# Moving the loads of attention's keys, values and queries from SyncE's queue to GpSimd's

## The chip, the cores and the metric

The kernel runs on one core of one Trainium2 chip. Times are device microseconds of a whole execution; the median of three runs is compared. A profiled execution gives, beside its own device time, a trace whose times count from the first instruction of the span.

## The reference

`q`, `k`, `v` are (8, 8, 576, 64) in float32: 8 sequences, 8 heads, 576 tokens, 64 columns. Retention (linear attention with a decay and no softmax) is followed by a feed-forward layer with a softplus:

```python
scores = q @ k.T / sqrt(64)
ret = (scores * Dmat) @ v            # Dmat[i, j] = gamma[h] ** (i - j) for i >= j, else 0
x = ret, its heads side by side      # 4608 tokens x 512
h = x @ w_in                         # 512 -> 2048
g = max(h, 0) + log1p(exp(-abs(h)))
out = g @ w_out                      # 2048 -> 512
```

## The kernel before

**Attention in steps.** The 4608 tokens are 36 chunks of 128. A step `m` is half a chunk's heads, so there are 72 steps, two to a chunk. A step's data are a `keys` tile (128x512 float32, 256 KB: the keys in two layouts) and a `qv` tile (128x640, 320 KB: queries and values). Steps 0 to 10 are loaded whole into tiles of their own. From step 11 on `load_keys` and `load_rest` issue two DMAs for each step, into two buffers for `keys` and two for `qv` (odd steps from 17 on have their `qv` in a pool named `odd`, so that there are then four).

**What a step does.** `chunk_products` gives TensorE a group of small 64x64 matmuls: scores (L204) and sums of key times value (L220) of the coming step or pair of steps, values (L282) and the terms from the running state (L294) of the one before. GpSimd copies half of the old state into `sx` (L259), multiplies the new state by its decay (L278) and scales the values of a loaded step by a power of gamma (L197, `scale_values`). L220 of a step reads those scaled values, so the order for a step is: load `qv`, land, L197, next group on TensorE. A buffer of `keys` or `qv` comes free when the group that reads it last has run.

**The feed-forward layer** is done for 512 tokens at a time (a unit), in float32 split into a high and a low part, three matmuls for one. Up to about 121 us `hidden_mm` (L453) and `output_mm` (L482) run while the weights arrive (`wst`). From then on the split weights, and sums of their blocks (Strassen's scheme: seven products for eight), lie in HBM, and each `product` (L830, six 128x512 matmuls) or `second` (L1117) takes its block from a ring of five buffers of 256 KB; `block_load` (L600) issues the load of the next block as soon as a product has been put out.

**Stages.** 42 to 121 us: hidden and output products beside the weights. 121 to 201 and 229 to 311 us: `plain_slot`, two products and a unit's outputs in each slot, a group of small matmuls in every second one. 201 to 229 and 325 to 463 us: `strassen_pair`, seven products, outputs and a group. About 517 to 624 us: the first `full_pair`s, seven products and one or two `second`s with a group in each. Then no attention is left.

**Order of issue.** Each engine runs its instructions in the order in which the program writes them. All DMAs are issued by SyncE (SP): loads of weights, ring blocks, `keys`, `qv`, and stores. In `plain_slot` the group's loads for the steps after (`next_steps`) are issued at once behind the group's matmuls. In `strassen_pair` and `full_pair`, `queue_steps` puts them into the list `queued`, of which each `product` issues one behind its ring block:

```python
load_keys(ks[0])
queued[:0] = [lambda: load_rest(ks[0]), lambda: load_rest(ks[1]), lambda: load_keys(ks[1])]
queued.append(lambda: [scale_values(k) for k in ks])
```

Of the kernel before, what the change touches and what calls it, by code (L numbers as in the profile page):

```python
# [34 lines left out]
KEYS = 4 * C  # L35
# [4 lines left out]
FIRST = AHEAD - 1  # L40
# [42 lines left out]
def retention_softplus_ffn(ctx: ExitStack, tc, first, whole, others, consts, w, out):  # L83
    nc = tc.nc
# [68 lines left out]

    def load_keys(m):
        keys = rawp.tile([P, KEYS], F32, tag="keys", name="keys")
        nc.sync.dma_start(keys, others[m - FIRST][:, 0:KEYS])
        loaded(m, k=keys[:, 0:2 * C], kp=keys[:, 2 * C:])

    def load_rest(m):
        place = later["odd"] if m >= 2 * CHUNKS - 1 and m % 2 else rawp  # L160
        qv = place.tile([P, RAW - KEYS], F32, tag="qv", name="qv")
        nc.sync.dma_start(qv, others[m - FIRST][:, KEYS:])
        loaded(m, q=qv[:, 0:-2 * C], v=qv[:, -2 * C:])

    def loaded(m, **tiles):
        live.setdefault(m, {}).update((n, x.rearrange("p (s c) -> p s c", s=2)) for n, x in tiles.items())

    def load_step(m):

        if m == 0:  # L170
            at = 0
            for x in parts:
                nc.sync.dma_start(x, first[:, at:at + x.shape[1]])
                at += x.shape[1]
            k, q = parts[0][:, 0:2 * C], parts[0][:, 2 * C:4 * C]
            kp, v = parts[1][:, 0:2 * C], parts[1][:, 2 * C:4 * C]
        else:
            if m < NOPEN:
                place = openp if m < OPEN1 else openp2
                r = place.tile([P, 8 * C if m < FIRST else RAW], F32, name=f"raw{m}")  # L180
                nc.sync.dma_start(r, whole[m - 1] if m < FIRST else others[m - FIRST])
                keys, qv = r[:, 0:KEYS], r[:, KEYS:]
            else:
                load_keys(m)
                load_rest(m)
                return
            k, kp, q, v = keys[:, 0:2 * C], keys[:, 2 * C:], qv[:, 0:-2 * C], qv[:, -2 * C:]
        live[m] = {n: x.rearrange("p (s c) -> p s c", s=2) for n, x in dict(k=k, q=q, kp=kp, v=v).items()}
# [543 lines left out]
    for i in range(NF):  # L732
        n = START_WEIGHTS + 2 * i
        m = AHEAD + (i - 1) // 2
# [72 lines left out]
    def queue_steps(steps):  # L807
        ks = [m + 2 for m in steps if m + 2 < NSTEP]
        if not ks:
            return  # L810
# [3 lines that stand above are left out]
# [560 lines left out]
```

## Time and profile before

| | us |
|---|---|
| median of three runs | 845.3 |
| the three runs | 843.07, 845.3, 846.12 |
| the profiled execution, device time | 844.79 |
| its span in the trace | 843.0 |
| TensorE busy in the span | 829.7 |
| GpSimd busy in the span | 157.5 |

The profiled execution took 1.79 us outside its span. TensorE's granted clock was 0.999 of full speed over the span. In the trace PE is TensorE's matmul, PEld its weight load, DVE VectorE, ACT ScalarE, POOL GpSimd and SPq SyncE's queue of DMA issues.

### The profile page before, as it was taken

Reading aid. Unit: us, or ns where it says so; the run is one execution under the profiler, and the core shown is the slowest. Engines: PE = TensorE matmul, PEld = TensorE weight load, DVE = VectorE, ACT = ScalarE, POOL = GpSimd, SP = SyncE. Lnnn points to the kernel's source line nnn. Section 1 sums busy time; section 2 is a strip of 40 time slices with the busy share of each in tenths; the row PEclk is TensorE's granted clock in tenths of the full one; section 3 lists DMA queues with packets and bytes.
Section 4 is the critical chain, followed back from the end, with each engine's and each line's share of the span. In section 5 each row is a group of like instructions: output and inputs, shape, how many; then the busy total and the mean of one; then the engine's idle time right before and its main releaser. Section 6 shows DMA issues by size and latency. Waiting matters only on the chain.

```text
span 843.0 us, 18984 instructions
## 1 busy us (share of the span) xinstructions
PE 829.7 (98%) x7370; PEld 674.8 (80%) x7370; DVE 602.4 (71%) x1024; ACT 536.2 (64%) x921; POOL 157.5 (19%) x212
## 2 busy tenths in 40 slices
PE   7999999999999999999999999999999999999998
PEld 6788888887888888888888888787778888888786
DVE  5999965876587667777775744877789955555875
ACT  6778754447654447667766436676775658878643
POOL 4322222440222441111101000112110002212100
PEclk9999999999999999999999999999999999999999
DMA  9898878656677763988789747879756676666665
GB/s 364 299 304 307 289 259 311 224 197 225 227 258 261 253 206 105 325 277 268 252 282 305 271 176 243 255 218 302 226 155 213 209 243 191 188 192 194 198 205 190
DMA packets 137481, 203.64 MB, mean 242 GB/s; under 512 B 10288, under 2 KB 99888, under 8 KB 137392
## 3 DMA queue, kind: packets, MB, share of 16 engines
q1 hardware_dynamic: 137392, 202.43, 72.6%
q8 instruction: 59, 0.97, 0.5%
q14 instruction: 30, 0.25, 0.1%
HBM read 156.25 MB, written 46.14 MB: 240 GB/s over the span
## 4 chain that ended last, share of the span: by engine, by line
PE 85%; DVE 5%; ACT 4%; DMA 3%; issue 1%; POOL 1%; SPq 0%; DVEq 0%; POOLq 0%; ACTq 0%
PE y L482 23%; PE acc L830 18%; PE sum L1117 12%; PE two L830 11%; PE h L453 4%; PE third L830 4%; PE third L220 2%; PE two L204 2%; PE two L1117 1%; PE two L282 1%; PE third L1117 1%; PE acc L1117 1%; DMA ring<-combined 1%; PE two L294 1%; DMA raw<-whole 1%
## 5 line engine op out<-in xcount | busy, mean ns | idle before, releaser
L482 PE MATMUL y<-wout,g 128*128 128x512 f32 x960 | 233.7, 392 | 0.2 <-DVE g L475 0.2
L482 PEld LDWEIGHTS y<-wout,g 128*128 128x128 f32 x960 | 178.5, 188 | 38.7 <-PE h L453 0.6
L830 PE MATMUL acc<-xt,ring 128*128 128x512 f32 x768 | 194.1, 391 | 0.4 <-DMA ring<-combined 0.2
L830 PEld LDWEIGHTS acc<-xt,ring 128*128 128x128 f32 x768 | 143.6, 188 | 32.7 <-ACT parts L1107 0.7
L830 PE MATMUL two<-xt,ring 128*128 128x512 f32 x480 | 122.4, 391 | 1.3 <-DVE quad L956 0.5
L1117 PE MATMUL sum<-parts,ring 128*128 128x512 f32 x480 | 118.1, 396 | 0.0
L830 PEld LDWEIGHTS two<-xt,ring 128*128 128x128 f32 x480 | 89.6, 188 | 22.0 <-ACT ab L1154 1.6
L1107 ACT CAST parts<-g 128x512 fp32r<-128x512 f32 x112 | 68.5, 621 | 60.0 <-PE sum L1117 19.4
L1117 PEld LDWEIGHTS sum<-parts,ring 128*128 128x128 f32 x480 | 89.1, 188 | 21.7 <-DMA ring<-outsplit 0.6
L1111 DVE TENSOR_TENSOR parts<-g,parts 128x512 fp32r<-128x512 f32 x112 | 78.0, 714 | 29.9 <-ACT parts L1107 28.6
L462 ACT ACTIVATE ab<-ab 128x512 f32<-128x512 f32 x128 | 81.0, 632 | 4.1
L463 ACT ACTIVATE ab<-ab 128x512 f32<-128x512 f32 x128 | 80.9, 632 | 4.1
L471 ACT CAST g<-ab 128x512 fp32r<-128x512 f32 x60 | 37.1, 619 | 57.5 <-DVE ab L467 35.8
L197 POOL TENSOR_TENSOR qv<-qv,consts_sb 128x256 f32<-128x256 f32 x61 | 45.7, 749 | 125.5 <-DMA qv<-others 125.5
L475 DVE TENSOR_TENSOR g<-ab,g 128x512 fp32r<-128x512 f32 x60 | 44.2, 737 | 16.2 <-ACT g L471 15.3
L259 POOL COPY sx<-s 64x256 f32<-64x256 f32 (+1 forms) x34 | 13.2, 389 | 207.6 <-PE third L220 161.2
L1127 DVE SCALAR_TENSOR_TENSOR g<-g,ab 128x512 f32<-128x512 f32 x64 | 45.2, 716 | 7.3 <-ACT ab L463 7.1
L453 PE MATMUL h<-xt,win 128*128 128x512 f32 x192 | 48.3, 400 | 1.0 <-DVE x L397 0.7
L278 POOL TENSOR_TENSOR s<-s,consts_sb 128x256 f32<-128x256 f32 (+1 forms) x31 | 20.3, 656 | 127.8 <-DVE s L276 111.7
L453 PEld LDWEIGHTS h<-xt,win 128*128 128x128 f32 x192 | 35.4, 188 | 9.6 <-ACT wout L563 0.8
L1213 POOL TENSOR_TENSOR g<-g 128x512 f32<-128x512 f32 x9 | 12.3, 1369 | 151.2 <-DVE g L1127 151.2
L461 ACT ACTIVATE ab<-quad 128x512 f32<-128x512 f32 x40 | 25.2, 631 | 23.4 <-DVE quad L956 12.0
(182 smaller groups left out, 1322.5 us busy)
## 6 DMA issues: line engine op xcount, KB each, us to landing
ring<-split SPq DMA_DIRECT2D x126, 256.0 KB, 3.9
ring<-combined SPq DMA_DIRECT2D x104, 256.0 KB, 3.6
qv<-others SPq DMA_DIRECT2D x61, 320.0 KB, 4.8
wst<-w SPq DMA_DIRECT2D x32, 512.0 KB, 5.8
ring<-outcombined SPq DMA_DIRECT2D x64, 256.0 KB, 3.4
keys<-others SPq DMA_DIRECT2D x61, 256.0 KB, 4.8
ring<-outsplit SPq DMA_DIRECT2D x48, 256.0 KB, 3.8
split<-win SPq DMA_DIRECT2D x16, 512.0 KB, 6.5
```

The lines of the kernel that those rows point to most:

```text
L197: nc.gpsimd.tensor_mul(v, v, f.unsqueeze(2).broadcast_to([P, 4, D]))
L453: nc.tensor.matmul(h, wins[p][:, a, kt * P:(kt + 1) * P], xt[:, b, T1 + kt // 2, kt % 2], start=(n == 0), stop=(n == 3 * NKT - 1))
L462: nc.scalar.activation(ab, ab, AF.Exp, scale=-1.0)
L463: nc.scalar.activation(ab, ab, AF.Ln, bias=1.0)
L471: nc.scalar.copy(g[:, HI], ab)
L475: nc.vector.tensor_sub(g[:, LO], ab, g[:, HI].bitcast(F32))
L482: nc.tensor.matmul(ys[u][tt], g[:, a, tt * P:(tt + 1) * P], wouts[p][:, b], start=(p == 0 and n == 0), stop=(p == NF - 1 and n == 2))
L830: nc.tensor.matmul(bank, w[:, ta, kt * P:(kt + 1) * P], xt[:, tb, x, kt], start=start and k == 0, stop=k == 5, skip_group_check=True)
L1107: nc.scalar.copy(t[:, HI], g_slot(J, n))
L1111: nc.vector.tensor_sub(t[:, LO], g_slot(J, n), t[:, HI].bitcast(F32))
L1117: nc.tensor.matmul(bank[m], w[:, a, m * P:(m + 1) * P], t[:, b], start=start and n == 0, stop=n == 2, skip_group_check=True)
L1127: nc.vector.scalar_tensor_tensor(c, c, 0.0, ab, op0=ALU.max, op1=ALU.add)
```

## The change

From step 11 on, the two loads of each step are issued by GpSimd instead of SyncE. The diff in full:

```diff
     def load_keys(m):
         keys = rawp.tile([P, KEYS], F32, tag="keys", name="keys")
-        nc.sync.dma_start(keys, others[m - FIRST][:, 0:KEYS])
+        nc.gpsimd.dma_start(keys, others[m - FIRST][:, 0:KEYS])
         loaded(m, k=keys[:, 0:2 * C], kp=keys[:, 2 * C:])
 
     def load_rest(m):
         place = later["odd"] if m >= 2 * CHUNKS - 1 and m % 2 else rawp
         qv = place.tile([P, RAW - KEYS], F32, tag="qv", name="qv")
-        nc.sync.dma_start(qv, others[m - FIRST][:, KEYS:])
+        nc.gpsimd.dma_start(qv, others[m - FIRST][:, KEYS:])
         loaded(m, q=qv[:, 0:-2 * C], v=qv[:, -2 * C:])
```

These are 122 DMAs, 61 of each kind. The order of instructions on TensorE, VectorE and ScalarE is the same before and after. Two places show what moves on the other two.

The first is GpSimd's order in the `full_pair` that begins at 534 us (tiles `keys_6539` and `qv_6553` are step 62's, `keys_6576` and `qv_6565` step 63's). Before:

```order
L259 COPY sx_6531<-s_6338 64x256
L278 TENSOR_TENSOR s_6536<-s_6536,consts_sb_101 128x256
L197 TENSOR_TENSOR qv_6553<-qv_6553,consts_sb_101 128x256
L197 TENSOR_TENSOR qv_6565<-qv_6565,consts_sb_101 128x256
L259 COPY sx_6721<-s_6536 64x256
```

After:

```order
L259 COPY sx_6531<-s_6338 64x256
L278 TENSOR_TENSOR s_6536<-s_6536,consts_sb_101 128x256
L156 DMA keys_6539<-others 128x512
L162 DMA qv_6553<-others 128x640
L162 DMA qv_6565<-others 128x640
L156 DMA keys_6576<-others 128x512
L197 TENSOR_TENSOR qv_6553<-qv_6553,consts_sb_101 128x256
L197 TENSOR_TENSOR qv_6565<-qv_6565,consts_sb_101 128x256
L259 COPY sx_6721<-s_6536 64x256
```

The four loads stand behind the state's decay L278, all in one piece. On SyncE, before, the same four loads stood one by one between ring blocks:

```order
L156 DMA keys_6539<-others 128x512
L600 DMA ring_6551<-combined2_1_124 128x2x256
L162 DMA qv_6553<-others 128x640
L600 DMA ring_6563<-combined2_1_124 128x2x256
L162 DMA qv_6565<-others 128x640
L600 DMA ring_6574<-outsplit3_138 128x2x256
L156 DMA keys_6576<-others 128x512
L600 DMA ring_6586<-split5_108 128x2x256
```

Of these rows only the four of the ring are left on SyncE.

The second place is the last `plain_slot` with a group, at 306 us, on GpSimd. After the change (before, the same rows without the four DMAs):

```order
L156 DMA keys_4001<-others 128x512
L162 DMA qv_4003<-others 128x640
L156 DMA keys_4005<-others 128x512
L162 DMA qv_4007<-others 128x640
L259 COPY sx_4009<-s_3844 64x256
L278 TENSOR_TENSOR s_4014<-s_4014,consts_sb_101 128x256
L197 TENSOR_TENSOR qv_4003<-qv_4003,consts_sb_101 128x256
L197 TENSOR_TENSOR qv_4007<-qv_4007,consts_sb_101 128x256
L434 TENSOR_TENSOR quad_4038<-xs_546 128x256
```

Here the four loads come ahead of `sx` and of the state's decay, and GpSimd's combinations of the next units' inputs (L434 to L437) stand last.

## Rows read from the trace of the kernel before

**Rows 1.** The profile's page, part 1 (busy us, share of the span, instructions of each engine) and the head of part 4 (the chain of work that ended last, share of the span by engine).
```profile
PE 829.7 (98%) x7370; PEld 674.8 (80%) x7370; DVE 602.4 (71%) x1024; ACT 536.2 (64%) x921; POOL 157.5 (19%) x212
...
PE 85%; DVE 5%; ACT 4%; DMA 3%; issue 1%; POOL 1%; SPq 0%; DVEq 0%; POOLq 0%; ACTq 0%
```

**Rows 2.** Who TensorE waited for between 42 and 843 us: us in total, times, longest us. The view has six rows; one of 0.4 us (ACT) and one of 0.7 us (issue) are left out.
```profile
PE third L220 <- DVE mark L336: 0.8, 2, 0.4
...
PE two L830 <- DVE quad L956: 0.5, 1, 0.5
...
PE two L830 <- DMA ring<-combined: 0.4, 1, 0.4
PE acc L830 <- DMA ring<-combined: 0.2, 1, 0.2
```

**Rows 3.** Busy time by stretch: us, then for each engine busy us (instructions), the granted TensorE clock, the DMA engines' share and GB/s.
```profile
42.00:121.00 79.00, 78.95 (x687) 63.36 (x687) 70.93 (x132) 61.28 (x107) 18.57 (x25) 1.00 0.84 287
...
517.00:610.00 93.00, 90.97 (x1162) 73.30 (x1163) 72.16 (x128) 66.61 (x115) 15.76 (x24) 1.00 0.79 253
```

**Rows 4.** Who SyncE's queue waited for before it issued a load of `keys`: us in total, times, longest us.
```profile
SPq L156 <- PE third L220: 22.6, 15, 2.5
```

**Rows 5.** The page, part 6: DMA issues, their count, KB each, median us from issue to landing.
```profile
ring<-combined SPq DMA_DIRECT2D x104, 256.0 KB, 3.6
qv<-others SPq DMA_DIRECT2D x61, 320.0 KB, 4.8
```

**Rows 6.** The view of the tile `qv`: SyncE's time for one issue (ns, min/median/max) and the time from issue to landing.
```profile
L162 SPq DMA_DIRECT2D qv<-others x61: 332/550/1979, 43.8 to 599.5; - x61
...
DMA to landing us min/median/max: 3.1/4.8/7.8
```

**Rows 7.** The timeline of GpSimd in the `full_pair` from 534 us: start us, us, instruction, [idle before <- what ended it].
```profile
534.70 0.39 POOL L259 COPY sx<-s 64x256 f32<-64x256 f32 x1 [4.85 <-PE third L220]
538.48 0.61 POOL L278 TENSOR_TENSOR s<-s,consts_sb 128x256 f32<-128x256 f32 x1 [3.38 <-DVE s L276]
...
543.27 0.66 POOL L197 TENSOR_TENSOR qv<-qv,consts_sb 128x256 f32<-128x256 f32 x1 [2.17 <-DMA qv<-others]
549.28 0.39 POOL L259 COPY sx<-s 64x256 f32<-64x256 f32 x1 [5.34 <-PE third L220]
```

**Rows 8.** The timeline of TensorE where the next group begins.
```profile
545.82 1.30 PE L830 MATMUL acc<-xt,ring 128*128 128x512 f32 x5
547.05 0.73 PE L204 MATMUL two<-qv,keys 64*64 64x64 f32 x21
```

**Rows 9.** The timeline of SyncE's queue in the same `full_pair`.
```profile
538.14 0.59 SPq L162 DMA_DIRECT2D qv<-others  x1
...
539.51 0.59 SPq L156 DMA_DIRECT2D keys<-others  x1
540.30 0.52 SPq L600 DMA_DIRECT2D ring<-split  x1
```

**Rows 10.** The chain of work that ended last, between 306 and 326 us: start us, us, what.
```profile
306.66 0.10 POOL sx L259
...
313.48 0.61 POOL qv L197
314.08 1.69 POOL quad L434
...
318.59 1.16 POOL quad L437
...
319.77 1.06 ACT xt L441
...
320.85 1.23 DVE xt L442
...
323.73 0.70 DVE quad L956
...
324.47 1.67 PE two L830 x6
```

**Rows 11.** The timeline of SyncE's queue, GpSimd and TensorE around the load of step 17's `qv`.
```profile
116.34 0.33 SPq L162 DMA_DIRECT2D qv<-others  x1
116.72 3.22 SPq L600 DMA_DIRECT2D ring<-split  x5
119.72 0.61 POOL L197 TENSOR_TENSOR qv<-qv,consts_sb 128x256 f32<-128x256 f32 x1 [6.65 <-DMA qv<-others]
...
120.99 0.24 PE L220 MATMUL third<-qv,keys 64*64 64x64 f32 x1
```

**Rows 12.** GpSimd's groups of instructions, shapes kept apart: count | busy us, mean ns of one.
```profile
L278 POOL TENSOR_TENSOR s<-s,consts_sb 128x256 f32<-128x256 f32 x24 | 15.3, 640 | 75.0 <-DVE s L276 67.4 <-DVE s L274 7.5
...
L434 POOL TENSOR_TENSOR quad<-xs 128x256 f32<-128x256 f32 x8 | 8.0, 994 | 0.0
```

**Rows 13.** The timeline of GpSimd: the state's decay L278 in the first, the fourth and the sixth `full_pair`, and the `sx` copies behind the fourth and the sixth.
```profile
522.93 0.61 POOL L278 TENSOR_TENSOR s<-s,consts_sb 128x256 f32<-128x256 f32 x1 [3.38 <-DVE s L276]
...
568.44 0.61 POOL L278 TENSOR_TENSOR s<-s,consts_sb 128x256 f32<-128x256 f32 x1 [3.38 <-DVE s L276]
...
579.27 0.39 POOL L259 COPY sx<-s 64x256 f32<-64x256 f32 x1 [5.36 <-PE third L220]
...
599.81 0.61 POOL L278 TENSOR_TENSOR s<-s,consts_sb 128x256 f32<-128x256 f32 x1 [3.38 <-DVE s L276]
...
610.62 0.39 POOL L259 COPY sx<-s 64x256 f32<-64x256 f32 x1 [5.35 <-PE two L294]
```

**Rows 14.** The timeline of GpSimd and TensorE in a `plain_slot`: the second scaling, a combination, and the group that reads the scaled values.
```profile
160.49 0.61 POOL L197 TENSOR_TENSOR qv<-qv,consts_sb 128x256 f32<-128x256 f32 x1 [0.98 <-DMA qv<-others]
161.06 1.18 POOL L434 TENSOR_TENSOR quad<-xs 128x256 f32<-128x256 f32 x1
...
162.53 0.27 PE L220 MATMUL third<-qv,keys 64*64 64x64 f32 x1
```

## The prediction, made before the changed kernel was run

> **What bounds the kernel now.** I read the page's shares and its chain first: TensorE is busy for 829.7 of 843.0 us and holds 85% of the chain that ended last, GpSimd 19% busy and 1% of the chain [rows 1]. So time can only be won or lost where TensorE stops. The waits of TensorE after 42 us are the next view: they come to some 3 us in all, and those that a DMA ended are 0.4 and 0.2 us, both for ring blocks [rows 2]. No wait of TensorE is for `keys` or `qv`. The table by stretch agrees: from 42 to 121 us TensorE is busy for 78.95 of 79.00 us, from 517 to 610 us for 90.97 of 93.00 [rows 3]. The reader should see that there is next to nothing to gain, and look for slack that the change could use up.
>
> **What the change takes away.** SyncE loses 122 issues of 0.55 us (median) [rows 6], and its waits ahead of them, of which the largest row is 22.6 us over 15 times [rows 4]. Behind those stood ring blocks and weight loads, which now go out earlier. That is worth at most what TensorE waited for the ring, 0.6 us [rows 2], and I count nothing for it: the chunk loads still move their bytes beside the ring's, and may make one of its blocks late as before.
>
> **What it adds.** GpSimd issues 122 DMAs, four in a row from the plain slots on. The trace has no DMA issued by GpSimd, so its price t, as time that GpSimd is held, must be bounded. Lower end: 0.33 us, SyncE's shortest issue of the same load; nothing at all is excluded, since the instruction has to be carried out in line. Upper end: 1.7 us, GpSimd's longest 128x256 instruction on the chain [rows 10]. Between them lie SyncE's median of 0.55 [rows 6] and GpSimd's own instructions, 0.64 (L278) and 0.99 (L434) on average [rows 12]. I take t = 1.0: the nearest rows are GpSimd's own, and an issue for 128 rows is more than a short elementwise instruction.
>
> The Trainium skill, DMA: Bandwidth & Descriptors, section "Latency and other measured facts", gives about 0.6 us to the first byte for a DMA of SyncE and about 1 us for one of GpSimd, whose cores write the descriptors in software. If only that difference of 0.4 us counted, each load would land 0.4 us later and the sum below would be smaller, about half a microsecond (an estimate from that page); no row here shows it.
>
> From the end of the issue to landing: SyncE's fastest is 3.1 less 0.33, some 2.8 us; its median 4.8 less 0.55, some 4.2 [rows 6], with other loads queued ahead. I take 3.5, the middle; ring blocks, of nearly the same size, land 3.6 us after issue [rows 5].
>
> **Where that meets slack.** GpSimd does its list in order, so I go through it by stage.
>
> From 42 to 116 us GpSimd issues two loads per step and has little else to do. They leave when the buffer comes free rather than behind weight loads, so they come no later; nothing.
>
> (a) *Step 17's `qv`*, the first into the memory that the weights leave. SyncE issues it at 116.34, it is scaled from 119.72 to 120.33, and TensorE starts the group at 120.99 [rows 11]: 0.66 us of slack. The memory comes free no earlier after the change, so it is 116.34 + 1.0 + 3.5 + 0.61 = 121.45, or 0.5 us late. The five ring loads, until now behind it, move beside it, a reason not to take less than 3.5.
>
> (b) *Plain slots.* Four issues come ahead of the `sx` copy and the state's decay, which are needed one group later, some 11 us on; that covers them. Without that cover it would be 4t a group. The loads themselves: in the tightest slot the second scaling ends at 161.10 and TensorE reads at 162.53 [rows 14], 1.4 us of slack. Against SyncE's issues (four of 0.55) the fourth leaves 4 x (1.0 - 0.55) = 1.8 us later, less what the queue in front then saves, 4.2 - 3.5 = 0.7: 1.1 us later. It just fits; nothing.
>
> The last plain slot has no slack. There the chain runs from the group's end on TensorE at 306.66 over the last `qv` load, its scaling at 313.48, GpSimd's combinations L434 to L437, ACT, DVE, and back to TensorE at 324.47 [rows 10], where TensorE already waits for that L956 [rows 2]. After: 306.66 + 4 x 1.0 + 3.5 = 314.16, 0.7 us later than 313.48, and TensorE with it.
>
> (c) *Strassen pairs and `full_pair`s.* Here the loads wait behind the decay L278. Of the two the `full_pair`s are tight. L278 ends at 539.09 [rows 7]; SyncE had issued the last `qv` at 538.14 and the last `keys` at 539.51 [rows 9]. Four issues end at 543.09, the last `keys` land at 546.6, the last `qv` (third) at 545.6, scaled by 546.3. TensorE starts the next group at 547.05 [rows 8]. 0.4 us to spare: nothing. Every issue over (547.05 - 539.09 - 3.5) / 4 = 1.1 us would stop TensorE in each such pair.
>
> Sum against the profiled execution: 844.79 + 0.5 (a) + 0.7 (b) = 846.0. It stands 0.5 below the median of its runs, so I forecast **846.5**, 0.14% slower, which a comparison of such runs cannot tell from no change; about 0.5% (4.2 us) is what can be told.
>
> **Rivals.**
>
> *GpSimd's issues are dear, and the next group waits* (slower). GpSimd's own instructions stretch: L434 takes 0.99 on average but 1.69 on the chain, next to a busy DVE [rows 10, 12]. If issues stretch alike, t = 1.7: from L278's start to the next `sx` copy there are 10.8 us in three `full_pair`s (538.48 to 549.28, 568.44 to 579.27, 599.81 to 610.62 [rows 7, 13]) and some 11.8 in the other three (522.93 to 534.70). The first three lose 4 x (1.7 - 1.1) = 2.4 us each, the others 1.4: 11.4. (b) becomes 3.5 and (a) 1.2, and plain slots lose a little each, so about 17 us: 862. With t = 1.4 it is 3 x 1.2 + 0.6 (others) + 2.3 + 0.9 = 7.4: 852.7. It decides from t = 1.25 on, where the sum passes 4.2 us. Against it: L278 itself, in the same place, shows 0.61 [rows 13]. The Trainium skill, SBUF — State Buffer, section "Who interferes with whom", names a mechanism: DMAs of GpSimd starve while DVE holds the port pair that both share with certain one-input instructions; by that rule t would swing with what DVE runs. The rows here show GpSimd's stretching, not its cause.
>
> *The four loads together starve the ring* (slower). They used to be spread over four products, now 1.15 MB goes out in 4t, beside ring blocks. In the `full_pair`s a product takes some 1.4 us and the ring is four ahead; a block that lands at the loads' pace (4.8 instead of 3.6 us [rows 5]) is 1.2 us later. If one in each of the six `full_pair`s that load were late by that, it would be 7.2 us: 852.5. Against it: the ring has waited behind the same bytes before and lost 0.6 us.
>
> *SyncE freed makes it faster.* All that TensorE waited for after 42 us is 3 us, the DMA part 0.6 [rows 2]: 844.7. It cannot pass 0.5%.
>
> **How the numbers follow.** Forecast 0.58; dear issues 0.27; starved ring 0.07; SyncE freed 0.08, of which I leave half to a gain that the view of waits does not show, and half is no change. So 0.04 faster, 0.62 same, 0.34 slower. The range runs from 843.5, all DMA waits gone and cheap issues, to 855, the ring's case and dear issues up to t = 1.5; about 0.17 is left outside, most of it above.
>
> **What would show it.** In the changed kernel's trace: GpSimd's DMA rows with their own time (about 1.0 us); the second L197 after 306 us starting near 314.2 and TensorE's L830 near 325; in the `full_pair`s the last scaling about 0.8 us ahead of the group. Waits of TensorE for POOL or for `qv` and `keys` in groups from 517 us on would show the first rival, with the price of an issue beside them; waits for ring blocks the second. I would be wrong if the landing after GpSimd's issue took much more than 3.5 us: each microsecond there weighs like 0.25 us of t.

## The result, and the profile after

The changed kernel takes 855.65 us (median of six runs, 853.26 to 857.33) against 845.5 us before (six runs, 843.07 to 846.12), a ratio of 1.0122 with a 95% interval of 1.0103 to 1.0141. It is 10 us slower; the forecast was 846.5, its range ended at 855.0. The profiled execution took 856.09 us, with a span of 854.4.

The page, parts 1 and 4 as in [rows 1]: TensorE's busy time has grown from 829.7 to 834.2 us, its share of the chain has fallen from 85% to 76%, and that of DMA has doubled.
```profile
PE 834.2 (98%) x7370; PEld 676.6 (79%) x7370; DVE 606.2 (71%) x1024; ACT 535.9 (63%) x921; POOL 223.5 (26%) x334
...
PE 76%; DVE 9%; DMA 6%; ACT 5%; issue 2%; POOL 1%; SPq 0%; DVEq 0%; ACTq 0%; POOLq 0%
```

Who TensorE waited for from 42 to 843 us (us in total, times, longest), as in [rows 2]. Waits for ring blocks were 0.6 us; now they are 5.4 + 0.6, and the 2.5 put down to DVE's L639 belong to them too, as the rows after next show. There is still no wait for `keys` or `qv`.
```profile
PE acc L830 <- DMA ring<-split: 5.4, 5, 2.6
PE acc L830 <- DVE quad L639: 2.5, 1, 2.5
PE two L830 <- DVE quad L956: 1.0, 2, 0.5
...
PE sum L1117 <- DMA ring<-outsplit: 0.6, 2, 0.4
```

The stretches of [rows 3] after: from 42 to 121 us TensorE is all but as busy as before (78.85 of 79.00 us), while from 517 to 610 us it is busy for 85.82 us instead of 90.97, and the DMA engines moved 221 GB/s instead of 253.
```profile
517.00:610.00 93.00, 85.82 (x1039) 68.31 (x1038) 67.05 (x116) 61.77 (x106) 23.73 (x42) 0.98 0.66 221
```

One `full_pair` shows what happens, the one of [rows 7 to 9]. First GpSimd's timeline (start us, us, instruction):
```profile
542.80 0.58 POOL L156 DMA_DIRECT2D keys<-others  x1
543.37 1.06 POOL L162 DMA_DIRECT2D qv<-others  x2
544.42 0.54 POOL L156 DMA_DIRECT2D keys<-others  x1
548.19 0.69 POOL L197 TENSOR_TENSOR qv<-qv,consts_sb 128x256 f32<-128x256 f32 x1 [3.23 <-DMA qv<-others]
549.54 0.72 POOL L197 TENSOR_TENSOR qv<-qv,consts_sb 128x256 f32<-128x256 f32 x1 [0.66 <-DMA qv<-others]
```
Then SyncE's issue of one ring block, the time from that issue to its landing (the view of line L600 at 544 us), that of the same block before the change (issued at 540.30 in [rows 9]), and TensorE's wait for it:
```profile
544.05 0.52 SPq L600 DMA_DIRECT2D ring<-split  x1
```
```profile
DMA to landing us min/median/max: 7.8/7.8/7.8
```
```profile
DMA to landing us min/median/max: 5.0/5.0/5.0
```
```profile
551.99 1.23 PE L830 MATMUL acc<-xt,ring 128*128 128x512 f32 x3 [2.50 <-DVE quad L639]
```
The ring block that left at 544.05 landed at 551.85, and TensorE went on at 551.99. The row names the combination L639, which ended just before, but the product does not need it: before the change the same product ran at 545.59, and L639 came after it, on VectorE:
```profile
547.29 0.42 DVE L639 TENSOR_TENSOR quad<-quad 128x256 f32<-128x256 f32 x1
```
Ring blocks take 3.4 to 4.4 us in the medians of the page; this one took 7.8, with four loads of GpSimd leaving around it. The loads themselves are late too, though no wait shows it: the second scaling ends at 550.26, but the last `keys`, issued at 544.42, took 7.2 us and landed at 551.64, hardly before the ring block.
```profile
DMA to landing us min/median/max: 7.2/7.2/7.2
```

Then a second cost comes, which the waits do not count. The granted clock of TensorE behind that wait, by stretches of 1 us (busy times, then the clock in the third column from the end):
```profile
552.00:553.00 1.00, 1.00 (x3) 0.78 (x4) 0.96 (x3) 0.00 (x0) 0.00 (x0) 0.72 0.56 180
553.00:554.00 1.00, 1.00 (x4) 0.66 (x2) 0.13 (x1) 0.00 (x0) 0.00 (x0) 0.50 0.09 29
554.00:555.00 1.00, 1.00 (x13) 0.57 (x14) 0.00 (x0) 0.46 (x1) 0.00 (x0) 0.50 0.01 2
555.00:556.00 1.00, 1.00 (x48) 1.00 (x47) 0.00 (x0) 0.97 (x3) 0.00 (x0) 0.57 0.04 11
```
After 2.5 us without work the clock fell to 0.50, the lower of its two levels (1.2 of 2.4 GHz). Over the four rows 0.28 + 0.50 + 0.50 + 0.43 = 1.71 us of full speed are lacking, so it was low for 3.4 us and TensorE lost some 1.7 on top of the wait. Not every such wait has this price: the longest of the trace, 2.6 us until 602.1, was followed by full clock.
```profile
602.00:603.00 1.00, 0.92 (x4) 0.83 (x5) 0.84 (x3) 0.00 (x0) 0.00 (x0) 1.00 0.41 135
```

**Where the 11.4 us between the spans lie.** The same instruction, after less before: 1.69 us by the first hidden product (rows below), 2.15 at step 17's group (123.14 - 120.99, [rows 11]), 2.53 at 324 us (327.00 - 324.47, [rows 10]), 3.21 at the first `full_pair`'s decay (526.14 - 522.93, [rows 13]) and 11.32 at the `sx` copy behind the sixth (621.94 - 610.62). So 8.1 us arose in the six `full_pair`s, 1.5 between 25 and 523 us, and 1.7 at the start. The last row, and the one at the first decay, after the change:
```profile
526.14 0.62 POOL L278 TENSOR_TENSOR s<-s,consts_sb 128x256 f32<-128x256 f32 x1 [3.39 <-DVE s L276]
```
```profile
621.94 0.39 POOL L259 COPY sx<-s 64x256 f32<-64x256 f32 x1 [4.29 <-PE two L294]
```
The waits add up to that: in the `full_pair`s TensorE waits 8.5 us for ring blocks (5.4 + 2.5 + 0.6 above) and loses 1.7 to the clock, and some 1.9 us that it waited there before are gone: 8.3, for the 8.1 of the spans.

The start is no part of the change. TensorE's first hidden product before, and after:
```profile
23.54 2.79 PE L453 MATMUL h<-xt,win 128*128 128x512 f32 x11 [0.66 <-DVE x L397]
```
```profile
25.23 3.03 PE L453 MATMUL h<-xt,win 128*128 128x512 f32 x12 [0.66 <-DVE x L397]
```
Among the kernels below this instruction started anywhere from 23.29 us (`paced`, all loads on GpSimd) over 25.08 (`only_full`, none on GpSimd until 517 us) to 25.83 (`act_spread`, none on GpSimd at all).

### The profile page after: what moved, and what is told of

Its sections match the earlier page's. It is cut to its first block, busy times and chain, and to the rows that moved or that the text cites. A ratio compares the mean times of both kernels' runs of the same rounds, so it can differ in the third digit from the quotient of the medians.

```text
span 854.4 us, 18928 instructions
## 1 busy us (share of the span) xinstructions
PE 834.2 (98%) x7370; PEld 676.6 (79%) x7370; DVE 606.2 (71%) x1024; ACT 535.9 (63%) x921; POOL 223.5 (26%) x334
## 4 chain that ended last, share of the span: by engine, by line
PE 76%; DVE 9%; DMA 6%; ACT 5%; issue 2%; POOL 1%; SPq 0%; DVEq 0%; ACTq 0%; POOLq 0%
PE acc L830 19%; PE y L482 18%; PE sum L1117 12%; PE two L830 10%; DMA ring<-split 4%; PE third L830 4%; PE two L1117 3%; PE third L220 2%; PE two L204 2%; DVE wst L551 1%; PE two L282 1%; DVE g L475 1%; PE acc L1117 1%; PE third L1117 1%; PE two L294 1%
## 5 line engine op out<-in xcount | busy, mean ns | idle before, releaser
L278 POOL TENSOR_TENSOR s<-s,consts_sb 128x256 f32<-128x256 f32 (+1 forms) x31 | 20.3, 654 | 104.3 <-DVE s L276 87.3
L156 POOL DMA_DIRECT2D keys<-others x61 | 34.3, 562 | 42.7 <-PE third L220 29.2
```

## The experiments

All are timed against the kernel before on the same chip; its medians there were 844.4 to 845.3 us. "Between 517 and 630 us" are the `full_pair`s. Steps 60 to 71 are loaded there.

### Where: late_sync and only_full

`late_sync`, and `only_full` with the condition turned round:
```diff
-        nc.gpsimd.dma_start(keys, others[m - FIRST][:, 0:KEYS])
+        (nc.gpsimd if m < 60 else nc.sync).dma_start(keys, others[m - FIRST][:, 0:KEYS])
```
and the same for `qv`.

> GpSimd issues the loads of steps 11 to 59, SyncE those of steps 60 to 71 (the full_pairs), as before the change. Theory A (the loss arises where four loads leave together beside the full_pairs' tight ring): the 8.3 us that TensorE lost between 517 and 612 us are gone, what is left is the shift of 2 to 3 us that the changed kernel shows before 517 us, so 846 to 848.5 us; no wait of TensorE over 0.3 us for a ring block in the full_pairs. Rival (GpSimd's loads cost something wherever they stand, by its issues or its queue): 850 us or more.

> SyncE issues the loads of steps 11 to 59, GpSimd only those of steps 60 to 71. Theory A: the whole loss of the full_pairs is there, 853 to 855 us, with TensorE waiting some 8 us for ring blocks between 517 and 612 us, and nothing lost before 517 us. If the first 42 us start as early as in the kernel before, the 1.7 us that the changed kernel lost there come from GpSimd's queue in use early; if they are late again, from the chance of a start or from the queue being there at all. Rival (cost wherever GpSimd issues): 847 us, a fifth of the loads having a fifth of the loss.

Measured: `late_sync` 847.52 us, ratio 1.0036 (1.0019 to 1.0053); `only_full` 855.89, ratio 1.0145 (1.0111 to 1.0178), a little more than expected. In `late_sync` the stretch from 517 to 610 us is as before (rows 3: 90.97):
```profile
517.00:610.00 93.00, 91.35 (x1070) 73.13 (x1069) 71.85 (x126) 66.65 (x115) 15.58 (x24) 1.00 0.76 248
```
Its two waits for ring blocks there, 0.5 and 0.3 us, are those of the kernel before in kind and size. What follows: 24 of the 122 loads, those of the `full_pair`s, make most of the loss. The other 98 cost 1.6 to 4.5 us.

### Four at once, or the queue: sync_burst, paced, gp_early, act_spread, sync_late

In `sync_burst` SyncE issues all loads, in the `full_pair`s the four in a row (against the kernel before):
```diff
         load_keys(ks[0])
-        queued[:0] = [lambda: load_rest(ks[0]), lambda: load_rest(ks[1]), lambda: load_keys(ks[1])]
+        if ks[0] >= 60:
+            for f in (lambda: load_rest(ks[0]), lambda: load_rest(ks[1]), lambda: load_keys(ks[1])):
+                f()
...
```
`paced` is the changed kernel with idle work ahead of the second, third and fourth load:
```diff
+        def apart(f):
+            if ks[0] >= 60:
+                for _ in range(4):
+                    t = rawp.tile([P, C], F32, tag="idle", name="idle")
+                    nc.gpsimd.memset(t, 0.0)
+            f()
-        queued[:0] = [lambda: load_rest(ks[0]), lambda: load_rest(ks[1]), lambda: load_keys(ks[1])]
+        queued[:0] = [lambda: apart(lambda: load_rest(ks[0])), lambda: apart(lambda: load_rest(ks[1])),
+                      lambda: apart(lambda: load_keys(ks[1]))]
```

> No load is issued by GpSimd. In the full_pairs SyncE issues the four loads in a row where the first of them stood before, not one by one between ring blocks. Theory A1 (four loads at once starve the ring, whoever issues them): the ring blocks behind the four land some 3 us late, 851 to 856 us. Theory A2 (it takes GpSimd's own queue, whose packets go ahead of the ring's in the DMA engines, or the later place in GpSimd's order): 845 to 848 us.

> The changed kernel, with four memsets of 128x128 on GpSimd (0.20 us each) between one load and the next in the full_pairs, so that the four leave some 1.35 us apart, about as far apart as SyncE issued them. Theory A1 (four at once): most of the 8.3 us comes back, 846 to 850 us, ring blocks at most 6.5 us from issue to landing. Theory A2 (GpSimd's queue itself): 853 to 857 us, ring blocks up to 8 us late as in the changed kernel.

Measured: `sync_burst` 849.37 us (847.06 to 853.41), ratio 1.0056 (1.0032 to 1.0079): between the two theories. `paced` 852.18, ratio 1.0097 (1.0080 to 1.0115): also between. Its loads left 1.1 to 1.5 us apart, and ring blocks still took up to 7.1 us. Its waits between 517 and 630 us, of which the second comes with the idle work (the last `keys` leave later and come too late):
```profile
PE acc L837 <- DMA ring<-split: 4.1, 5, 1.5
PE third L220 <- DMA keys<-others: 2.1, 2, 1.8
PE sum L1124 <- DMA ring<-outsplit: 1.5, 1, 1.5
```
So the bunching is part of it: four in a row on the ring's own queue already cost 4.9 us (849.37 against 844.43), about half of the loss. But neither theory holds alone. Three runs took place and queue apart. `gp_early` puts GpSimd's loads ahead of the decay (against the changed kernel):
```diff
             chunk_products(*group)
+            ks = next_steps(group[0])
             group_out(*group, between=(finish,))
-            queue_steps(group[0])
+            queued.append(lambda: [scale_values(k) for k in ks])
```
`act_spread` gives the `full_pair`s' loads to ScalarE, one behind each product (against the kernel before, `qv` alike):
```diff
-        nc.sync.dma_start(keys, others[m - FIRST][:, 0:KEYS])
+        (nc.scalar if m >= 60 else nc.sync).dma_start(keys, others[m - FIRST][:, 0:KEYS])
...
```
`sync_late` leaves them with SyncE, three products later (against the kernel before):
```diff
+        gap = 3 if ks[0] >= 60 else 0
...
+            queued[:0] = [lambda: None] * gap + [lambda: load_keys(ks[0])]
```

> The changed kernel, but in the full_pairs GpSimd issues the four loads right behind the group's matmuls, ahead of the sx copy and of the state's decay L278, so about where SyncE issued its first one and some 4 us sooner than in the changed kernel; still four in a row on GpSimd's queue. Theory P (the loss comes from the later place behind the decay, so that the loads meet the ring where its reserve is used up): 847 to 849 us. Theory Q (on GpSimd's own queue the loads pass the ring blocks that were issued before them): 851 to 856 us, and ring blocks of 6 us or more from issue to landing that left before the loads did.

> No load is issued by GpSimd. In the full_pairs ScalarE issues the four loads, one by one at the places where SyncE did, on a queue of its own. Theory Q (loads on another queue than the ring's pass ring blocks issued before them): ring blocks of 6 us and more from issue to landing in the full_pairs, 848 to 853 us. Rival (it takes GpSimd's software-made packets, or the later place): 845 to 847 us, if ScalarE's four issues of some 0.5 us per full_pair stay hidden.

> No load is issued by GpSimd. In the full_pairs SyncE issues the four loads one by one between ring blocks as in the kernel before, but three products (some 4 us) later, about where GpSimd issued them. Theory P (the later place makes the loss): 850 to 855 us. Theory Q (GpSimd's own queue makes it): 845 to 847.5 us, ring blocks at most 6 us from issue to landing.

Measured: `gp_early` 856.69 us, ratio 1.0128 (1.0101 to 1.0155); `act_spread` 854.17, ratio 1.0104 (1.0070 to 1.0139); `sync_late` 870.86, ratio 1.0299 (1.0247 to 1.0351).

`gp_early` differs from the changed kernel in the place alone and is no faster, so the place behind the decay is not the cause (theory P falls); it stands 0.7 us above the range of theory Q. It issues from 521.05 us on in the first `full_pair`, `sync_burst` from 519.79: nearly the same place, the same four in a row, another queue, and 7.3 us between them. Not all of these belong to the queue in the `full_pair`s, since `gp_early` has the other 98 loads on GpSimd too (1.6 to 4.5 us by `late_sync`). `only_full` leaves those with SyncE as `sync_burst` does: it is 6.5 us slower, and the two intervals lie apart. So a queue of its own costs more than the bunching alone. The wait row of `gp_early`, and the clock in one of the 6.8 us that it stayed low around the end of a wait of 2.9 us at 530.94:
```profile
PE acc L830 <- DMA ring<-combined: 7.0, 3, 3.0
```
```profile
531.00:532.00 1.00, 1.00 (x3) 0.81 (x4) 0.00 (x0) 0.00 (x0) 0.00 (x0) 0.50 0.59 204
```
`act_spread`, 1.2 us above the range of theory Q, shows that it need not be GpSimd: ScalarE's loads do the same from a hardware queue. They were to be spread and are bunched as well (it comes to them at 538.78 to 540.51 in the second `full_pair`). The other 98 loads stay with SyncE here too, and it stands 4.8 us above `sync_burst`, though these two intervals overlap. The queues of the DMA engines from 539.8 to 546.9 us (records, each a packet that one engine moved, MB, share of the 16 engines' time; q10 is ScalarE's, q1 SyncE's), and the ring block issued there at 540.04:
```profile
q10 hardware_dynamic: 570, 1.17, 54.9%
q1 hardware_dynamic: 1092, 1.06, 43.3%
...
ring<-combined SPq DMA_DIRECT2D x1, 256.0 KB, 7.9
```
That block landed at 547.95. ScalarE's last load, issued after it at 540.51, had landed by then, at 547.62 (the view of its line):
```profile
DMA to landing us min/median/max: 7.1/7.1/7.1
```
`sync_late` lies outside both expectations, since the loads come too late for their own group. Its waits between 517 and 630 us:
```profile
PE third L220 <- DMA keys<-others: 7.3, 4, 1.9
PE third L220 <- POOL qv L197: 7.2, 5, 2.2
PE two L204 <- DMA keys<-others: 3.0, 1, 3.0
```
Its total therefore tells nothing of place against queue. That no ring block is among the waits is no test either: TensorE stood for the loads for 17.5 us in all, time in which the ring could fill.

### How the queues share: wide_gp, act_wide, burst_wide, wide_sync

The ring's blocks are laid out in HBM so that a partition's part is one piece of 2 KB; the rest of each kernel is as named (the changed kernel, `act_spread`, `sync_burst`, the kernel before).
```diff
-    split = [dram.tile([P, 2, PIECE], F32R, name=f"split{p}") for p in range(NF)]
+    split = [dram.tile([P, 2, 2, 2 * P], F32R, name=f"split{p}") for p in range(NF)]
...
-            nc.sync.dma_start(t.bitcast(F32), s[:, :, n * 2 * P:(n + 1) * 2 * P].bitcast(F32))
+            nc.sync.dma_start(t.bitcast(F32), s[:, n].bitcast(F32))
...
```

> The changed kernel with the ring's blocks laid out in HBM so that each partition's 2 KB of a block stand in one piece, not in two of 1 KB (so 128 packets for a block where there were 256; stores of such tiles and the loads of whole ones become two DMAs of one half each). Theory Q1 (the two queues take turns packet by packet, so that the ring with 1 KB packets gets a small share beside loads of some 3.7 KB a packet): the ring gets about twice the share while loads run, the loss in the full_pairs falls from 8 us to 3 to 5, 848 to 852 us. Theory Q2 (the loads go first whatever the packets, or place and burst alone decide): 854 to 857 us.

> The kernel in which ScalarE issues the four loads of a full_pair on its own queue (854.2 us), with the ring's blocks in pieces of 2 KB. Theory Q1: ring packets then take 84 ns beside load packets of 84 to 102, not 46, so of two queues in turn the ring has about 47% instead of 33%; the loss falls from 9 us to 3 to 6, 848 to 851 us, and the longest time from issue to landing of a ring block falls from 7.9 to below 7 us. Theory Q2 (a second queue goes ahead whatever its packets): 853 to 856 us.

> The kernel in which SyncE issues the four loads of a full_pair in a row (849.4 us), with the ring's blocks in pieces of 2 KB. On one queue the ring's blocks wait for the bytes ahead of them, however they are cut. Theory Q1: 848 to 850 us, as without the wide layout. Rival R (wide blocks simply arrive sooner): 845 to 846.5 us.

> The kernel before (all loads on SyncE, one by one) with the ring's blocks in pieces of 2 KB in HBM instead of 1 KB. Theory Q1 (the wide layout helps only where two queues take turns packet by packet): 843.5 to 845.5 us, no difference that can be told. Rival R (wide blocks simply arrive sooner, and that alone gave back the 4 us in the changed kernel with wide blocks): the 3 us that TensorE lost to waits between 517 and 630 us go too, 841 to 842.5 us.

Measured, with 1 KB beside it:

| loads in the `full_pair`s | 1 KB pieces | 2 KB pieces | ratio to before at 2 KB |
|---|---|---|---|
| GpSimd's queue | 855.65 | 851.17 | 1.0090 (1.0058 to 1.0121) |
| ScalarE's queue | 854.17 | 850.01 | 1.0063 (1.0035 to 1.0092) |
| SyncE's, in a row | 849.37 | 850.41 | 1.0061 (1.0040 to 1.0082) |
| SyncE's, one by one | 844.8 (before) | 846.33 | 1.0013 (0.9999 to 1.0026) |

`wide_sync` and `burst_wide` came out 0.8 and 0.4 us above their ranges, the other two within theirs (the longest landing of a ring block in `act_wide` is 6.7 us, below 7 as expected). By the medians wide pieces give some 4 us back where the loads have a queue of their own, and nothing where they share the ring's. Each of the two gains alone is not clear of the noise, since the ratios at 1 KB are 1.0122 (1.0103 to 1.0141) and 1.0104 (1.0070 to 1.0139) and the intervals overlap with those at 2 KB. The traces bear them out: from the first `sx` copy of the `full_pair`s to the last, this stretch is 8.1 us longer than before in the changed kernel and 4.2 in `wide_gp`, 9.8 in `act_spread` and 4.7 in `act_wide`. The queues from GpSimd's first load record to its last in the first `full_pair`, of the changed kernel and of `wide_gp`:
```profile
q0 software_dynamic: 318, 1.18, 62.9%
q1 hardware_dynamic: 577, 0.56, 33.1%
```
```profile
q0 software_dynamic: 317, 1.18, 53.1%
q1 hardware_dynamic: 463, 0.85, 41.8%
```
While the same 1.18 MB of loads passed, the ring got 0.56 MB in 5.0 us with 1 KB pieces, and 0.85 in 6.0 with 2 KB. Its share goes with the size of its pieces, which speaks for engines that serve both queues piece by piece, not by bytes or by the order of issue. The worst moment of the changed kernel, from 529.5 to 531 us, shows how little is left to the ring (a record counts whole where it starts, so the shares can pass 100%):
```profile
q0 software_dynamic: 130, 0.51, 91.1%
q1 hardware_dynamic: 72, 0.06, 12.8%
```
The Trainium skill, DMA: Bandwidth & Descriptors, section "Queues, rings and completion order", says that each DMA engine goes round the queues that have work and changes only between packets. The rows agree with that in kind; strict turns of one record each they do not show (577 records of the ring to 318), so what a turn holds stays open.

### The ring's reserve, and the bytes: ring6_gp, ring6_sync, half_gp

```diff
-RING = 5
+RING = 6
...
-        qv = place.tile([P, RAW - KEYS], F32, tag="qv", name="qv")
+        n = 4 * C if place is not rawp else RAW - KEYS
+        qv = place.tile([P, n], F32, tag="qv", name="qv")
...
```
on the changed kernel and on the one before. Both leave out the queries' second copies in the odd steps and read other columns in their place, so what they put out is not the reference's result; they serve for the time alone. And `half_gp` is the kernel before with only the `qv` loads on GpSimd:
```diff
-        nc.sync.dma_start(qv, others[m - FIRST][:, KEYS:])
+        nc.gpsimd.dma_start(qv, others[m - FIRST][:, KEYS:])
```

> The changed kernel with six ring buffers instead of five. To make room, odd steps from 17 on load only 512 of the 640 columns of their qv (queries' second copies are left out and the values read other columns), so 64 KB less of the 1152 KB of a full_pair; the instructions are the same. Theory S (a ring block that the loads pass is late by a fixed time, and TensorE loses what exceeds the ring's reserve): one product, 1.36 us, comes off each of the eight stalls of the changed kernel's full_pairs (0.35 to 2.75 us), which leaves some 3 of the 9.8 us and no fall of the clock there, 847 to 850 us. Rival (the ring is short of bytes over the whole pair, a deeper one starves as well): 853 to 857 us.

> The kernel before with six ring buffers, the same columns left out. All theories: TensorE lost 3 us to waits between 517 and 630 us, so 842.5 to 845.5 us.

> GpSimd issues only the qv loads (640 of the 1152 KB of a full_pair), SyncE the keys, between ring blocks as before. Theory S: some 0.55 of the bytes pass the ring at once, a block is late by 1.5 us less than in the changed kernel, and the loss falls from 10 to 3 to 6 us: 848 to 851 us. Rival (it takes any load on a second queue, however small): 853 us or more.

Measured: `ring6_gp` 845.42 us, ratio 1.0004 (0.9992 to 1.0015); `ring6_sync` 843.04, ratio 0.9972 (0.9959 to 0.9985); `half_gp` 854.52, ratio 1.0111 (1.0093 to 1.0129). With a sixth buffer the changed kernel is as fast as the one before, more than expected. Against `ring6_sync`, its own partner, 2.4 us of the 10 are left. The waits of `ring6_gp` between 517 and 630 us, and the landing of its slowest ring block:
```profile
PE acc L831 <- DMA ring<-split: 1.7, 1, 1.7
PE third L221 <- DMA keys<-others: 1.0, 1, 1.0
```
```profile
DMA to landing us min/median/max: 8.3/8.3/8.3
```
Its blocks are as late as in the changed kernel (up to 8.3 us here, 8.1 there); TensorE just meets them one product later. So what it loses is the delay beyond the reserve of five buffers, and there the loss is settled. With all columns loaded a sixth buffer lacks about 0.5 KB per partition; a complete kernel with six was not tried, and no complete kernel here beats the one before.

`half_gp` lies in the range of the rival. SyncE's row in the first `full_pair`, and the landing of the ring block of 526.41, offer another reason than the rival's: the second `keys` went out just ahead of it on its own queue, so it had 256 KB ahead of it and 640 beside it, nearly what the four loads were.
```profile
525.62 0.59 SPq L156 DMA_DIRECT2D keys<-others  x1
```
```profile
DMA to landing us min/median/max: 8.1/8.1/8.1
```
It was no test of fewer bytes; whether the delay goes with the bytes that pass stays open.

## Why the prediction was wrong, by its own steps

**What bounds the kernel: right.** TensorE bounds it, there was nothing to gain, and no wait for `keys` or `qv` came up. It named the `full_pair`s as the tight stage, and that was where the time went. The forecast of 846.5 us and the range failed by one term, (c), which stood at 0 and measured 8.1 us.

**The price of an issue, t = 1.0 us: nearly twice what it was.** GpSimd's 122 issues, by line (ns, min/median/max):
```profile
L156 POOL DMA_DIRECT2D keys<-others x61: 536/577/706, 40.6 to 611.8; - x61
...
L162 POOL DMA_DIRECT2D qv<-others x61: 536/536/544, 41.3 to 611.3; - x61
```
That is SyncE's median of 0.55, one of the rows that bounded it, and not GpSimd's elementwise instructions. The rival "dear issues" is out with it. The Trainium skill, SBUF — State Buffer, section "Who interferes with whom", says that VectorE can keep GpSimd from making the descriptors of its DMAs. No such stretching shows in these rows: the medians are 0.54 and 0.58 us and the longest issue 0.71.

**The landing, 3.5 us after the issue: too short.** The page gives, from the start of the issue:
```profile
qv<-others POOLq DMA_DIRECT2D x61, 320.0 KB, 5.0
...
keys<-others POOLq DMA_DIRECT2D x61, 256.0 KB, 4.5
```
so 4.4 and 3.9 after the issue of 0.54 to 0.58 us. In (a) and (b) the two errors offset each other; in (c) they do not.

**(a) Step 17's `qv`, +0.5 expected.** The memory came free at 118.69, the scaling began 3.79 us later, and TensorE started at 123.14. That is 0.53 us after the start of its last product (122.61), where it was 0.44 before (120.55 to 120.99), so (a) cost 0.1.
```profile
118.69 0.54 POOL L162 DMA_DIRECT2D qv<-others  x1 [3.01 <-DVE wout L568]
122.48 0.61 POOL L197 TENSOR_TENSOR qv<-qv,consts_sb 128x256 f32<-128x256 f32 x1 [3.25 <-DMA qv<-others]
```
```profile
123.14 0.27 PE L220 MATMUL third<-qv,keys 64*64 64x64 f32 x1
```

**(b) The last plain slot, +0.7 expected.** From the first issue to the second scaling 7.37 us, against 6.82 before (306.66 to 313.48 in [rows 10]): 0.55 later. TensorE's shift grew from 2.15 at 123 us to 2.53 here.
```profile
308.68 0.58 POOL L156 DMA_DIRECT2D keys<-others  x1 [2.70 <-PE third L220]
...
316.05 1.55 POOL L197 TENSOR_TENSOR qv<-qv,consts_sb 128x256 f32<-128x256 f32 x1 [0.83 <-DMA qv<-others]
```

**(c) The `full_pair`s, 0 expected: the step that failed.** Its sum followed only the loads, and what it did not follow is what they do to others: they made the ring late, and that cost the 8.1 us. The step "What the change takes away" put it so: the loads "still move their bytes beside the ring's, and may make one of its blocks late as before". But it was not as before, in two ways. Four loads leave at once, which costs 4.9 us even on the ring's queue (`sync_burst`). And on that one queue a ring block waited only for loads issued ahead of it, while from a queue of their own loads issued after a block land before it (`act_spread`), and GpSimd's pieces are larger than the ring's, which costs it more of the engines' time (`wide_gp`).

For the loads too the sum held by luck. From the start of the decay to the next group it had 8.57 us (538.48 to 547.05 in [rows 7 and 8]) and expected the last `keys` after 8.1. They landed after 9.4 (542.24 to 551.64), since beside the ring the landing took 7.2 us. TensorE did not wait for them because it was standing for the ring block until 551.99. In `ring6_gp`, where it stands less, such a wait of 1.0 us appears.

**The rival "the four loads together starve the ring" was the mechanism,** given 0.07 and 852.5 us. Its 7.2 us come near the 8.1, but not by its own sum: it took one block in each `full_pair` to be 1.2 us late. The one of 544.05 was 2.8 us later than before (7.8 instead of 5.0), and 2.5 of them became a wait. The eight waits in six pairs run from 0.2 to 2.6 us. Two terms were missing: the clock's fall behind a wait, and the waits of the kernel before that fall away. "The ring has waited behind the same bytes before and lost 0.6 us" was the argument against it, and it held for spread loads on one queue only. The 0.6 us were in truth the warning: TensorE waited 0.4 and 0.2 us for ring blocks already [rows 2], so there the reserve was nil before the change, and whatever made a block later would be paid in full.

**The rival "SyncE freed"** gave nothing that the rows show.

**What stays open.** `late_sync` is 3.1 us slower than before (1.6 to 4.5), the rows of (a) and (b) account for some 0.6 of it, and `ring6_gp` stands 2.4 above `ring6_sync`. Where the rest lies no run here settles. How the loss of the `full_pair`s divides between four loads at once and the second queue is known only roughly: about half each by the medians (4.9 us in `sync_burst`, 9.3 in `act_spread`, 11.5 in `only_full`).

## What to carry to other kernels

Loads on one queue keep their order, so a stream with a deadline waits only for what was put ahead of it; a second queue takes that away, and the more so the larger its pieces are beside the stream's. Loads issued in one go cost the stream time on either queue here. Before a load is moved to a queue of its own, look at the waits for what stays behind: a small wait there is no sign of a small effect but of an empty reserve, which one more buffer can restore. Behind a long wait of TensorE look at the granted clock too: here one of 2.5 us cost 1.7 more, and one of 2.6 us nothing.

## What was unexpected of the hardware

- GpSimd's DMA issue for 128 rows took 0.54 to 0.58 us in the median, as SyncE's did (0.55), and went out in larger pieces: 318 records for 1.18 MB, where ScalarE's queue needed 570 for as much.
- In one stretch of 1.5 us the ring's queue got 12.8% of the DMA engines' time and GpSimd's 91.1%, with three ring blocks under way.
- TensorE's granted clock fell to 0.50 around the end of waits of 2.5 and 2.9 us, for 3.4 and 6.8 us, but not after the one of 2.6 us in the same trace as the first. It can be low at the start too: in `act_spread` it was 0.50 from 8 to 14 us, where in the kernel before it was 1.00.
- The Trainium skill, DMA: Bandwidth & Descriptors, section "Issuing engines are not separate DMA queues", holds that DMAs from several engines interleave on the same 16 engines, and that this saves only the time of issuing. The first half agrees with the rows (577 records of the ring beside 318 of GpSimd's in one stretch). The second falls short here: a second queue also cost time, 6.5 us in `only_full` over `sync_burst`, since the interleaving takes the ring's place in line.
